# Order of batch 5's loads, casts and transposes in a fused sparse attention and squared-ReLU kernel

## The chip, the cores and the metric

The kernel runs on one NeuronCore of a Trainium2 chip. The metric is the device time of one execution in microseconds (us). The profile names the engines PE (TensorE matmuls), PEld (TensorE weight loads), DVE (VectorE), ACT (ScalarE), POOL (GpSimd) and SP (SyncE, which here only issues DMAs).

## What is computed

Attention over q, k and v of 8 batches, 8 heads, 576 positions and 64 columns (float32), with a sparse mask; then a feed-forward block over all 4608 tokens. Heads 0 to 3 are "local": a position sees itself and the 31 before it. Heads 4 to 7 are "strided": a position sees the earlier ones that are a multiple of 32 away.

```python
scores = scale * np.matmul(q, k.transpose(0, 1, 3, 2))
rel = pos[:, None] - pos[None, :]
mask_local = (rel >= 0) & (rel < stride)
mask_strided = (rel >= 0) & (pos[None, :] % stride == pos[:, None] % stride)
# softmax over the masked scores, then attn @ v
x = np.ascontiguousarray(attn_out.transpose(0, 2, 1, 3)).reshape(B * S, H * D)
h = x @ w_in            # 4608 x 512 by 512 x 2048
r = np.maximum(h, 0.0)
return ((r * r) @ w_out).astype(np.float32)
```

## The kernel before

**Units and chunks.** Two heads of one batch are a unit: unit 4b + p holds heads 2p and 2p + 1 of batch b. Units 4b and 4b + 1 are local, 4b + 2 and 4b + 3 strided. The attention of a unit writes its 576 columns of xt[p], the transposed input of the feed-forward block. The block runs over nine chunks of 512 tokens. Chunk c has 16 groups mm1 (line 538: four matmuls of 512 columns, then Relu on ACT, then the square on DVE at line 555) and 16 groups mm2 (line 559: four matmuls; after each fourth group the sum is copied to y and stored).

**The order.** It is written out by hand: the program lists groups of matmuls, 32 for each chunk from chunk 3 on (mm1 of chunk c and mm2 of chunk c - 1 in turn). Ahead of a group, the attention steps that are due by then are emitted: step_SS (line 374) makes the scores of two units at once into six PSUM banks, step_D (line 469) multiplies by v, step_E (line 502) transposes into xt. Then come the hooks of that group, placed with at(n, fn) (line 803): loads, casts and transposes that feed later attention steps. Each engine runs its own instructions in the order in which they were emitted, and waits only for what it reads or overwrites. So a hook's group number sets its place in each queue, not its time.

**Batches from LB = 5 on.** Their operands are made without PE. For the local units, load_qk_local (line 108) loads q and k in float32 from SP, two DMAs of 144 KB for each tensor and unit; cast_qk_local (line 137) casts them to bf16 on POOL; transpose_local (line 196) transposes them with DMAs from SP into qT and kTl. For the strided units, cast_str_dram (line 165) casts q and k of four heads with DMAs issued from POOL into a DRAM scratch (q_d, k_d), and transpose_str (line 173) transposes that from SP into strT tiles (qT_s, kT_s). load_v_str_sw (line 229) brings strided v, in bf16, from POOL; cast_v_str (line 245) copies it on DVE into the layout that PE reads. loads_v (line 689) loads local v from SP into vl_st and casts it on POOL into vl.

**The hold.** hold_pool (line 676) copies one element of a tile named by came[b] on POOL. It computes nothing: POOL's later instructions, DMA issues included, wait until that tile is written. transpose_str sets came[b] to an element of the strided transposes of batch b.

**Where batch 5's hooks stand.** plan (line 806) works out g = 68 for batch 5, with g0 = 60, g1 = 78 and n0 = 80. Groups 64 to 79 are mm1 of chunk 2; from 80 on, mm1 of chunk 3 and mm2 of chunk 2 alternate.

| group | hooks of batch 5 before |
|---|---|
| 68 | loads_qk: SP loads q, k of units 20 and 21; POOL: hold for batch 4's strided transposes, q_d, k_d, strided v, four local casts |
| 76 | strided transposes (SP) |
| 79, 81 | local transposes of unit 20, of unit 21 (SP) |
| 80 | local v loads (SP) and casts (POOL) |
| 92, 93 | casts of strided v (DVE) |

The first reader of batch 5's local operands is step_SS(20), ahead of group 99; of its strided ones step_SS(22), ahead of group 114. step_D(18, 2) stands ahead of group 97. Batch 6's loads_qk stands at group 96, its local transposes at 110 and 114, step_SS(24) at 130.

Of the kernel before, what the change touches and what calls it, by code (L numbers as in the profile page):

```python
# [14 lines left out]
def kernel(  # L15
# [9 lines left out]
    nc = tc.nc  # L25
# [73 lines left out]
    units = [(b, p) for b in range(B) for p in range(H // 2)]  # L99
# [5 lines left out]
    LB = 5  # L105
    PAIRS = (10, 14, 18, 20, 22, 24, 26, 28, 30)

    def load_qk_local(u, eng, gate=None):
        b, p = units[u]
        s = st.setdefault(u, {})  # L110
        for name, src in (("q", q), ("k", k)):
            t = qk_st.tile([QL, 2, 6 * D], FP32, name=f"{name}_st")
            if gate is not None and name == "q":
                nc.gpsimd.tensor_copy(t[0:1, 0, 0:1], gate)
            if b >= LB:
                for hh in range(2):
                    eng.dma_start(out=t[:, hh].rearrange("p (t d) -> p t d", d=D),
                                  in_=src[b, 2 * p + hh].rearrange("(t p) d -> p t d", p=QL))
                s[name + "f"] = t
                continue  # L120
            eng.dma_start(out=t, in_=src[b, 2 * p:2 * p + 2]
                          .rearrange("h (p j) d -> p h (j d)", j=6))
            s[name + "f"] = t
# [13 lines left out]
    def cast_qk_local(u, copies, names="qk"):  # L137
        s = st[u]
        for name, copy in zip("qk", copies):
            if name not in names:  # L140
                continue
            t = qk_in.tile([QL, 6, 2, D], BF16, name=f"{name}_l")
            copy(t.rearrange("p j h d -> p h j d"),  # L143
                 s[name + "f"].rearrange("p h (j d) -> p h j d", j=6))
            s[name] = t
# [17 lines left out]
    came = {}  # L163

    def cast_str_dram(b):
        for name, src in (("q", q), ("k", k)):
            t = dram.tile([4 * SP_, NJ * D], BF16, name=f"{name}_d")
            nc.gpsimd.dma_start(
                out=t.rearrange("(x y) c -> x (y c)", x=16),
                in_=src[b, H // 2:H].rearrange("h (x y) d -> (h x) (y d)", x=4))  # L170
            big[b, name] = t

    def transpose_str(b):
        for name in "qk":
            o = strT.tile([128, NJ // 2, 4 * SP_], BF16, name=f"{name}T_s")
            nc.sync.dma_start_transpose(out=o, in_=big.pop((b, name)))
            came[b] = o[0:1, 0, 0:1]
            for i in range(2):
                st.setdefault(4 * b + 2 + i, {})[name + "T"] = o[:, :, 2 * SP_ * i:2 * SP_ * (i + 1)]
# [16 lines left out]
    def transpose_local(u):  # L196
        s = st[u]
        for name in "qk":
            if name == "k":
                full = kTl[v_slot(u)]  # L200
                dst = full[:, 32:32 + S]
            else:
                full = dst = qkT.tile([128, S], BF16, name="qk"[u % 2] + "T")
            nc.sync.dma_start_transpose(out=dst.rearrange("c (t p) -> c t p", p=QL),
                                        in_=s[name].rearrange("p t h d -> p (t h d)"))
            s[name + "T"] = full

    def v_slot(u):
        b, p = units[u]
        return (b * 2 + p % 2) % NV  # L210
# [18 lines left out]
    def load_v_str_sw(b):  # L229
        t = v_st.tile([SP_, 2, NJ * D], FP32, name="v_st")  # L230
        t = t.rearrange("p h c -> p (h c)").bitcast(BF16).rearrange("p (h c) -> p h c", h=4)
        nc.gpsimd.dma_start(out=t, in_=v[b, 4:8].rearrange("h (p j) d -> p h (j d)", j=NJ))
        for i in range(2):
            st.setdefault(4 * b + 2 + i, {})["vf"] = t[:, 2 * i:2 * i + 2]
# [10 lines left out]
    def cast_v_str(u, copy):  # L245
        s = st[u]
        t = vss[v_slot(u)]
        copy(t[:, :, 0:D], s["vf"].rearrange("p h (j d) -> p (h j) d", d=D))
        s["v"] = t
# [413 lines left out]
    pool2 = (nc.gpsimd.tensor_copy, nc.gpsimd.tensor_copy)  # L663
# [12 lines left out]
    def hold_pool(b):  # L676
        nc.gpsimd.tensor_copy(held, came[b])  # L677

    def loads_qk(b):
        for i in range(2):  # L680
            load_qk_local(4 * b + i, nc.sync)
        if b == LB:
            hold_pool(b - 1)
        cast_str_dram(b)
        load_v_str_sw(b)
        for i in range(2):
            cast_qk_local(4 * b + i, pool2)

    def loads_v(b):
        for i in range(2):  # L690
            load_v_local(4 * b + i, nc.sync)
        for i in range(2):
            cast_v_local(4 * b + i)
# [109 lines left out]
    def at(n, fn):  # L803
        hooks.setdefault(n, []).append(fn)

    def plan(b, g0, g1, n0=None):
        if b < LB:
            at(g0, lambda: transpose_str(b))
            for i in range(2):
                copies = dve2 if b == 2 else (nc.scalar.copy, nc.vector.tensor_copy)  # L810
                at(g1 + (4 if b > 2 else 2) * i, lambda u=4 * b + i, c=copies: cast_qk_local(u, c))
            return
        g = g0 + (g1 - g0) * 45 // 100
        g += 4 if b == 6 else 0
        tr, tl = max(g + 8, g0 + (g1 - g0) * 8 // 10), (g + 11, g + 13) if b == LB else (g + 14, g + 18)
        at(g, lambda: loads_qk(b))
        at(tr, lambda: transpose_str(b))
        at(n0, lambda: loads_v(b))
        for i in range(2):
            at(n0 + (12 if b == LB else 4) + i, lambda u=4 * b + 2 + i: cast_v_str(u, nc.vector.tensor_copy))  # L820
            at(tl[i], lambda u=4 * b + i: transpose_local(u))

    def second(n, *fns):
# [27 lines left out]
    rows = lambda b: (lambda: load_qk_local_sw(b, (4 * b, 4 * b + 1)))  # L851
    second(14, rows(2), lambda: load_v_local_sw(2), lambda: load_v_str_sw(2), lambda: cast_str_dram(2))
    plan(2, 28, 32)
    second(35, lambda: hold_pool(2), rows(3), lambda: load_v_local_sw(3), lambda: load_v_str_sw(3), lambda: cast_str_dram(3))
    for b, n in ((2, 36), (3, 56), (4, 75)):
        for i in range(2):
            second(n + i, lambda u=4 * b + 2 + i: cast_v_str(u, nc.vector.tensor_copy))
    for t in vl_sts:
        second(35, lambda t=t: nc.gpsimd.memset(t[0:32], 0.0))
    done_prev, g_prev = 0, 32  # L860
    plan(3, 42, 46)
    second(53, lambda: hold_pool(3), rows(4), lambda: load_v_local_sw(4), lambda: load_v_str_sw(4),
           lambda: cast_str_dram(4))
    plan(4, 64, 63)
    for b in range(2, B):
        g_end, s_end = ready.get(b, starts[b]), ends[4 * b + 3]
# [55 lines left out]
```

## Time and profile before

| what | value |
|---|---|
| median of 4 runs | 305.68 us (304.6 to 306.0) |
| profiled execution, its own time | 305.17 us |
| its span | 303.4 us |
| DVE, ACT, POOL busy | 158.1, 164.7, 63.2 us |
| DMA engines busy | 7 to 9 tenths or more up to about 182 us, then 0 to 3 tenths |
| step_SS(20) starts on PE | 125.91 us |
| step_SS(22), step_SS(24) start on PE | 140.97, 156.48 us |

The span is the time from the first to the last instruction of the program. A line of a group names the source line, the engine, the operation and out<-in by the program's tile names. "SPq" is the SP queue: the time of an issue there includes what SP waited for. Times in a timeline are from the span's start. A DMA's landing time is counted from its issue.

### The profile page before, as it was taken

How to read it: one execution, taken by the hardware profiler on the slowest of the kernel's cores; microseconds unless marked ns; L12 is line 12 of the kernel's file. 1: busy time of each engine (PE TensorE's matmuls, PEld its weight loads, DVE VectorE, ACT ScalarE, POOL GpSimd, SP SyncE). 2: the span in 40 equal slices, each digit the busy share in tenths (PEclk: the TensorE clock that was granted, in tenths of full speed). 3: DMA queues.
4: the chain of work that ended last, by engine and by line, in shares of the span. 5: the costliest groups of instructions: out<-in, count | busy, mean ns of one | idle time of the engine just before them, and what ended most of it. 6: DMA issues, size and time to landing. Idle time of an engine off the chain costs nothing.

```text
span 303.4 us, 6112 instructions
## 1 busy us (share of the span) xinstructions
PE 296.8 (98%) x2384; PEld 149.3 (49%) x2384; DVE 158.1 (52%) x418; ACT 164.7 (54%) x327; POOL 63.2 (21%) x94
## 2 busy tenths in 40 slices
PE   7989999999999999999999999999999999999996
PEld 2644454545555554555455545544444444444444
DVE  4557653768768967476747686374422222222200
ACT  4748738788477765555555456553344443444311
POOL 8853330080420321604332121000000000000000
PEclk9999999999999999999999999999999999999999
DMA  8999999799999999989899983122221001000122
GB/s 157 160 201 202 191 205 200 182 174 147 153 206 191 186 165 174 191 171 198 189 181 195 162 177 106 51 72 64 81 63 37 35 35 38 35 35 35 44 97 70
DMA packets 86317, 39.85 MB, mean 131 GB/s; under 512 B 70065, under 2 KB 80817, under 8 KB 86097
## 3 DMA queue, kind: packets, MB, share of 16 engines
q0 software_dynamic: 27520, 15.87, 38.4%
q1 hardware_dynamic: 58768, 23.60, 37.1%
q8 instruction: 18, 0.29, 0.4%
q14 instruction: 11, 0.08, 0.1%
HBM read 37.63 MB, written 13.57 MB: 169 GB/s over the span
## 4 chain that ended last, share of the span: by engine, by line
PE 93%; DMA 4%; POOL 1%; DVE 1%; issue 0%; SPq 0%; DVEq 0%
PE ph L546 35%; PE ph L583 35%; PE pt L546 6%; PE pt L583 3%; PE pt L486 3%; DMA w_in_b<-in_moe_w_in_dram 3%; PE py L583 2%; PE pt L404 2%; DMA k_st<-in_k_dram 1%; PE pt L284 1%; PE pt L569 1%; PE pt L340 1%; PE pt L522 1%; PE py L486 1%; PE pt L462 0%; POOL vl L240 0%
## 5 line engine op out<-in xcount | busy, mean ns | idle before, releaser
L546 PE MATMUL ph<-xt,w_in_b 128*128 128x512 bf16 x488 | 123.4, 379 | 0.0
L583 PE MATMUL ph<-w_out_b,g_sb 128*128 128x512 bf16 x480 | 123.0, 379 | 0.0
L555 DVE TENSOR_TENSOR g_sb<-r 128x512 bf16<-128x512 bf16 x144 | 62.1, 433 | 102.0 <-ACT r L552 101.2
L552 ACT ACTIVATE r<-ph 128x512 bf16<-128x512 f32 x122 | 72.6, 597 | 76.3 <-PE ph L546 73.4
L546 PEld LDWEIGHTS <-w_in_b 128*128 128x128 bf16 x576 | 52.8, 98 | 57.0 <-DMA w_in_b<-in_moe_w_in_dram 0.8
L583 PEld LDWEIGHTS <-g_sb 128*128 128x128 bf16 x560 | 51.1, 98 | 55.2 <-issue 0.4
L486 PEld LDWEIGHTS <-e 128*128 128x128 bf16 (+1 forms) x384 | 20.2, 97 | 14.4
L319 ACT ACTIVATE e<-pt 128x288 bf16<-128x288 f32 (+1 forms) x52 | 18.4, 410 | 7.5 <-PE pt L340 7.4
L416 ACT ACTIVATE e<-pt 72x504 bf16<-72x504 f32 (+3 forms) x45 | 20.8, 502 | 2.7 <-PE pt L404 2.7
L552 ACT ACTIVATE r<-pt 128x512 bf16<-128x512 f32 x21 | 12.2, 604 | 18.1 <-PE pt L546 18.1
L587 ACT COPY y<-ph 128x512 f32<-128x512 f32 x30 | 17.6, 587 | 7.2 <-PE ph L583 7.2
L546 PE MATMUL pt<-xt,w_in_b 128*128 128x512 bf16 x84 | 21.4, 379 | 0.0
L499 DVE TENSOR_TENSOR x_s<-pt,rinv 72x384 bf16<-72x384 f32 (+1 forms) x30 | 15.0, 500 | 1.0
L499 DVE TENSOR_TENSOR x_l<-pt,rinv 96x384 bf16<-96x384 f32 x23 | 12.7, 554 | 0.8
L498 DVE RECIPROCAL rinv<-pt 96x6 f32<-96x6 f32 (+2 forms) x53 | 9.8, 184 | 4.2 <-PE pt L486 4.0
L420 DVE TENSOR_TENSOR e<-e,mask_str 72x576 bf16<-72x576 bf16 x24 | 10.3, 449 | 2.5 <-ACT e L416 2.5
L583 PE MATMUL pt<-w_out_b,g_sb 128*128 128x512 bf16 x48 | 11.2, 379 | 0.0
L223 POOL CAST vl<-vl_st 128x768 bf16<-128x768 f32 x6 | 5.5, 920 | 26.1 <-DMA vl_st<-in_v_dram 25.9
L143 POOL CAST q_l<-q_st 96x768 bf16<-96x768 f32 x6 | 4.9, 825 | 26.0 <-DMA q_st<-in_q_dram 19.6
L677 POOL COPY held<-kT_s 1x1 bf16<-1x1 bf16 x3 | 0.6, 196 | 45.5 <-DMA kT_s<-k_d 45.5
L486 PE MATMUL pt<-vs,e 72*128 72x65 bf16 x156 | 9.3, 193 | 0.0
L354 DVE TENSOR_TENSOR e<-e,mask_full 128x576 bf16<-128x576 bf16 x16 | 7.2, 450 | 2.1 <-ACT e L319 1.9
(131 smaller groups left out, 245.4 us busy)
## 6 DMA issues: line engine op xcount, KB each, us to landing
out_dram<-y SPq DMA_DIRECT2D x35, 256.0 KB, 2.4
w_out_b<-in_moe_w_out_dram POOLq DMA_DIRECT2D x4, 512.0 KB, 14.1
v_st<-in_v_dram POOLq DMA_DIRECT2D x6, 288.0 KB, 9.6
q_d<-in_q_dram POOLq DMA_DIRECT2D x6, 288.0 KB, 7.4
k_d<-in_k_dram POOLq DMA_DIRECT2D x6, 288.0 KB, 8.9
q_st<-in_q_dram SPq DMA_DIRECT2D x12, 144.0 KB, 8.5
k_st<-in_k_dram SPq DMA_DIRECT2D x12, 144.0 KB, 3.8
vl_st<-in_v_dram SPq DMA_DIRECT2D x12, 144.0 KB, 2.9
```

The costliest lines, as they stand in the source:

```text
L319: nc.scalar.activation(e[0:kn, lo:lo + S // 2], pss[row][half][0:kn, 0:S // 2], AF.Exp, scale=scale)
L354: nc.vector.tensor_tensor(x, x, m, op=ALU.mult)
L416: nc.scalar.activation(o, x, AF.Exp, scale=scale)
L420: nc.vector.tensor_tensor(x, x, mask_full if local else mask_str.to_broadcast([kn, n, w]), op=ALU.mult)
L486: nc.tensor.matmul(po[:, n - n0, :], e[0:kn, pos(n):pos(n) + 128], rhs[0:kn, src(n), 0:D + 1], start=True, stop=True)
L498: nc.vector.reciprocal(rinv[0:w, 0:m], po[0:w, 0:m, D:D + 1])
L499: nc.vector.tensor_tensor(x, po[0:w, 0:m, 0:D], rinv[0:w, 0:m].to_broadcast([w, m, D]), op=ALU.mult)
L546: nc.tensor.matmul(ph, w_in_b[:, kk, 128 * ff:128 * (ff + 1)], xt[kk][:, 512 * c:512 * (c + 1)], start=(kk == order[0]), stop=(kk == order ...
L552: nc.scalar.activation(r, ph, AF.Relu)
L555: later(1, lambda: nc.vector.tensor_tensor(g[:, ff, :], r, r, op=ALU.mult))
L583: nc.tensor.matmul(py, g[:, ff, 128 * j:128 * (j + 1)], w_out_b[:, ff, :], start=(ff == 0), stop=(ff == 15))
L587: nc.scalar.copy(y, py)
```

## The change

For batch 5 alone, the strided loads leave loads_qk and become a hook of their own. The local casts come first on POOL, and the local transposes go to groups 72 and 74, ahead of the strided ones on SP. The hold now waits for batch 5's own local transposes (transpose_local sets came) instead of batch 4's strided ones, at group 75, and the strided loads follow it. The strided transposes go from group 76 to 80, where they stand ahead of the local v loads. The two casts of strided v on DVE go from groups 92 and 93 to 96 and 97. Batches 6 and 7 keep their order: loads_str stands where its two calls stood.

```diff
@@ transpose_local
             s[name + "T"] = full
+        came[units[u][0]] = full[0:1, 32:33]
@@ loads_qk
     def loads_qk(b):
         for i in range(2):
             load_qk_local(4 * b + i, nc.sync)
-        if b == LB:
-            hold_pool(b - 1)
+        if b > LB:
+            loads_str(b)
+        for i in range(2):
+            cast_qk_local(4 * b + i, pool2)
+
+    def loads_str(b):
         cast_str_dram(b)
         load_v_str_sw(b)
-        for i in range(2):
-            cast_qk_local(4 * b + i, pool2)
@@ plan
         g += 4 if b == 6 else 0
-        tr, tl = max(g + 8, g0 + (g1 - g0) * 8 // 10), (g + 11, g + 13) if b == LB else (g + 14, g + 18)
+        tr, tl = max(g + 8, g0 + (g1 - g0) * 8 // 10), (g + 14, g + 18)
+        if b == LB:
+            tl, tr = (g + 4, g + 6), g + 12
+            at(g + 7, lambda: hold_pool(b))
+            at(g + 7, lambda: loads_str(b))
         at(g, lambda: loads_qk(b))
         at(tr, lambda: transpose_str(b))
         at(n0, lambda: loads_v(b))
         for i in range(2):
-            at(n0 + (12 if b == LB else 4) + i, lambda u=4 * b + 2 + i: cast_v_str(u, nc.vector.tensor_copy))
+            at(n0 + (16 if b == LB else 4) + i, lambda u=4 * b + 2 + i: cast_v_str(u, nc.vector.tensor_copy))
             at(tl[i], lambda u=4 * b + i: transpose_local(u))
```

## The prediction

> **What bounds the kernel now.** I read the busy times on the page first, then TensorE's (PE's) own waits, then the chain of work that ended last, and only then the queues that the edit touches (SP, POOL, DVE) around 100 to 130 us.
>
> ```profile
> PE 296.8 (98%) x2384; PEld 149.3 (49%) x2384; DVE 158.1 (52%) x418; ACT 164.7 (54%) x327; POOL 63.2 (21%) x94
> ```
>
> PE is busy for 296.8 of 303.4 us. The view of waits, PE alone, says what the rest is: who waited, for whom, us in total, times, longest.
>
> ```profile
> PE py L603 <- DVE xt L700: 1.3, 1, 1.3
> PE py L546 <- DMA w_in_b<-in_moe_w_in_dram: 0.5, 1, 0.5
> PE pt L462 <- DVE xt L464: 0.5, 1, 0.5
> PE pt L340 <- DVE kTl L299: 0.5, 1, 0.5
> PE ph L284 <- ACT q_l L143: 0.4, 1, 0.4
> PE pt L522 <- DVE xt L464: 0.2, 1, 0.2
> ```
>
> That is all, and PE's timeline places every one before 20.3 us; the rest of the missing time is the last eviction and store after 300.5 us. But a busy PE may hide waits, because matmul ends are modelled. So I looked at starts, in the chain (start, us, what), close to where batch 5 is first used:
>
> ```profile
> 118.76 0.86 PE ph L583 x4
> 119.63 0.86 PE ph L546 x4
> 120.49 0.86 PE ph L583 x4
> 121.35 0.86 PE ph L546 x4
> ```
>
> Four matmuls of 512 columns in 0.86 us, and the next four begin 0.86 us after: no hole. Where attention steps lie between two groups, the extra 0.2 to 0.7 us is their own matmuls. So the stretch from 20.3 to 300.5 us is PE's own work, in PE's own order; the edit changes none of it. A gain there has nothing to remove. What the edit can do is to make PE wait. The question is which operand comes late.
>
> The queues now. SP first (start, us, operation):
>
> ```profile
> 99.87 2.04 SPq L117 DMA_DIRECT2D q_st<-in_q_dram  x2
> ...
> 104.28 4.81 SPq L117 DMA_DIRECT2D k_st<-in_k_dram  x2
> 109.20 3.85 SPq L176 DMA_TRANSPOSE qT_s<-q_d  x1
> ...
> 121.27 1.22 SPq L204 DMA_TRANSPOSE kTl<-k_l  x1
> ```
>
> and batch 5's first reader on PE, with the DVE work just ahead of it:
>
> ```profile
> 123.54 0.56 DVE L499 TENSOR_TENSOR x_s<-py,rinv 72x384 bf16<-72x384 f32 x1
> 124.80 0.43 DVE L555 TENSOR_TENSOR g_sb<-r 128x512 bf16<-128x512 bf16 x1 [0.70 <-ACT r L552]
> 125.14 0.17 DVE L498 RECIPROCAL rinv<-pt 72x4 f32<-72x4 f32 x1
> 125.34 0.42 DVE L499 TENSOR_TENSOR x_s<-pt,rinv 72x256 bf16<-72x256 f32 x1
> ```
> ```profile
> 125.91 0.43 PE L404 MATMUL pt<-qT,kTl 64*128 64x96 bf16 x12
> ```
>
> The last local transpose is issued at 121.27 and lands 2.6 us later at the earliest (the kTl tile's view: 2.6/2.7/3.7 min/median/max), at 123.9. PE reads it at 125.91: 2.0 us to spare. That is the tightest operand of the three batches. The same sum gives 148.56 + 2.7 = 151.3 against 156.48 for batch 6 (5.2 spare) and 173.05 + 3.7 = 176.8 against 181.82 for batch 7 (5.1).
>
> **What the Trainium skill says.** "TensorE: Matmul & The Clock Gate", section "Wait — 56ns, not 53.3ns?": a warm 512-column bf16 matmul follows its neighbour after 215.7 ns. The chain agrees: 0.86 us for four is 215 ns each, so PE runs at its rate. "Perfetto Trace Analysis", section "Tensor Engine Instruction (MATMUL, LD_WEIGHTS)": the profiler estimates TensorE ends; hence the check on starts. "DMA: Bandwidth & Descriptors", section "Queues, rings and completion order": the DMA engines take turns between queues with work, whoever issued it. The trace agrees: the first local q loads of batch 5 are cast 5.0 us after their issue (99.87 to 104.87, no wait), while those of batch 6, issued 1.6 us after the strided DMAs, wait until 136.48, 10.1 us. Same page, section "Two DMAs through the same engine are not ordered": the issuing engine waits on a semaphore before it issues a dependent DMA. So a transpose whose source is late holds all of SP behind it; one such wait of 2.4 us on q_d is in SP's waits.
>
> **The change, part by part.**
>
> (1) Hold and strided DMAs (q_d, k_d, v_st: 0.5 + 0.5 + 0.77 us of POOL) leave their place ahead of the local casts. POOL had idled 17.15 us to 102.65 in the old hold. The q and k loads of unit 20 land as before: casts at 104.87 and 106.25. Unit 21's loads no longer share the DMA engines. A q or k pair is 295 KB; at 205 GB/s, which the table by window shows for 99 to 101 us, it takes 1.4 us, so they land at about 107.7 and 109.1 (before: cast at 113.26 and 114.35). Last cast done 110.0.
>
> (2) Local transposes ahead of the strided ones on SP: four issues of 1.2 to 1.8 us behind the casts; the last at 110.3, landed at 112.9 to 114.0. I take 113.4. The spare time at 125.91 grows from 2.0 to about 12 us. Worth nothing to PE, which did not wait there.
>
> (3) New hold: POOL waits for that landing, 0.2 us, then issues q_d 113.6, k_d 114.1, v_st 114.6. Before: 103.10, 103.58, 104.09. So 10.5 us later. Batch 5's own times to landing, in the list of DMA issues for that window, are 5.4, 6.3 and 8.4 us; batch 6's v_st takes 9.6, and the longest of all six 13.4. With no local loads beside them but two DMA transposes: q_d 119.0, k_d 120.4, v_st 123.0 to 124.2. I take 123.5.
>
> (4) The DVE cast of v_st is put off by four groups, to the place after the x_s of 123.54, so DVE reaches it at 124.1. Two casts of 0.42 us go into idle time of 0.70 us (ahead of 124.80) and 0.88 us (ahead of 126.65); they cost nothing if v_st is there. Behind a blocked first cast are queued a g_sb square and then the rinv and x_s that empty the PSUM bank which the second half of PE's step at 125.91 writes, at 126.18. x_s ends at 125.76. So the cast may end as late as 124.8 without moving anything and about 125.2 without holding PE; v_st must land by 124.8. Spare: 1.3 us.
>
> (5) SP at the strided transposes waits for q_d: 119.0, then 1.3 to 3.9 us for the first and 1.3 for the second, say to 123.2. Needed at 140.97: no cost. But queued behind them, same group: the four vl_st loads. Before at 117.64, now 123.2: landed and cast from 126.9, against 121.33. The first reader of vl is PE at 135.93; unit 20's cast ends at 128.7. Spare 7 us.
>
> (6) What else is queued behind. On SP: two xt transposes, two output stores, then batch 6's loads, at about 129.3 instead of 126.42 (+2.9). The second xt transpose goes out at 127.5; even with the 8.5 us that it takes now it lands at 136.0, and PE needs it at 139.31. The stores hold two of four y buffers; no one asks for the fifth before 137. On POOL: batch 6's strided DMAs behind the vl casts, 130.4 instead of 124.82 (+5.6); v_st lands 131.4 + 9.6 = 141.0, DVE casts it at 144.47. Batch 6's last local transpose lands 24.9 us after its first load now; 129.3 + 24.9 = 154.2 against 156.48, spare 2.3. Batch 7 inherits at most the 2.9: 179.7 against 181.82, spare 2.1; its vl casts 184.6 against 188.12.
>
> Sum on PE's path: 0 + 0 + 0. The profiled execution took 305.17 us (span 303.4, 1.8 around it); the median of the four runs is 305.68, so nothing added to that is 305.6 in round numbers.
>
> **The rivals.**
> (A) No change, as above: 305.6.
> (B) Slower: v_st blocks DVE at 124.1, and DVE holds PE's bank. It decides from a landing after 125.2, 1.7 us beyond my estimate, and costs PE what goes beyond. For it: three DMAs behind a hold behind four transposes behind four casts, each of which can slip; at an issue of 115.6 and 11.2 us (between 9.6 and 13.4) it lands at 126.8: +1.6, 307.2. The worst, 114.6 + 13.4 = 128.0, gives +2.8, 308.4. Against: the 13.4 is from early in the kernel, beside weight loads.
> (C) Slower, later: the delay of 2.9 us on SP grows past 5 us and batches 6 or 7 miss their local transposes. At 6.5 us it costs 1.4: 307.0. Against: the SP queue drains between the batches.
> (D) Faster: the unprofiled runs are 0.5 us above the profiled one because PE sometimes does wait at 125.91; then the 10 us of new spare time removes that: 305.68 - 0.5 - some start-up luck, 304.7 at the lowest run's level. Against: 2.0 us spare in the trace.
> (E) The edit doesn't reorder what it says: the hold could fall through. It names an element of the tile that unit 21's transpose writes, so it waits; same time as A.
>
> **How the numbers follow.** A with E 0.65, B 0.17, C 0.10, D 0.08. A change under 0.3% (0.9 us) is about what a measurement of this kernel can tell from none. Some of A's own range is start-up: the runs go from 304.6 to 306.0. B and C give 0.27 for slower, D 0.08 for faster. To leave no more than 2 in 10 out, the range goes from 304.8 to 307.2; the likeliest case's own is 304.8 to 306.5.
>
> **What would show it.** Right: POOL's local casts without the wait ahead of 113.26, all done by 111; the hold ending at 113 to 114; no PE wait after 20.3 us; DVE's v_st casts at 124.1 and 125.8. Step 3 is wrong if v_st lands after 125: a wait of DVE on v_st and a hole in PE at 126. Step 6 is wrong if batch 6's first local matmuls start later than 30.6 us after batch 5's. And if the time falls by over 0.9 us, my reading that PE never waits is wrong.

## The result, and the profile after

| | before | after |
|---|---|---|
| median | 305.33 us (304.55 to 307.24, 49 runs) | 306.07 us (304.74 to 307.75, 30 runs) |
| profiled execution, its own time | 305.17 us | 306.15 us |
| its span | 303.4 us | 304.4 us |

The ratio is 1.0022, with a 95% interval of 1.0011 to 1.0032: slower by 0.7 us. That is small, and it is inside the range that was forecast, but the forecast was that PE's path gains and loses nothing. It lost something. (The prediction had four runs of before, with a median of 305.68 us; 49 give 305.33.) Here and below, a ratio and its interval leave out executions in a slower state of the chip (two of the 18 of the first experiment, 310.46 and 311.07 us), and they are not the quotient of the two medians. The profiled execution of after has 1.0 us more than its counterpart, so this pair of traces can show where time is lost.

First the busy times of the page of after, the row that the prediction shows for before:

```profile
PE 297.7 (98%) x2384; PEld 149.8 (49%) x2384; DVE 159.2 (52%) x418; ACT 164.5 (54%) x327; POOL 63.5 (21%) x94
```

PE has the same 2384 instructions and DVE the same 418, yet DVE is busy 1.1 us longer, 159.2 against 158.1. The same instructions took more time. PE's own waits in after (who waited, for whom, us in total, times, longest) have two entries past the start-up, where before had none, and both name DVE (the lines named here are one higher in after than in before):

```profile
PE pt L405 <- DVE x_l L500: 0.4, 1, 0.4
PE ph L547 <- DVE xt L531: 0.3, 1, 0.3
```

PE's timeline places them (start, us, instruction, idle time before it and what ended it):

```profile
108.66 0.38 PE L547 MATMUL ph<-xt,w_in_b 128*128 128x512 bf16 x1 [0.33 <-DVE xt L531]
...
111.75 0.43 PE L405 MATMUL pt<-qT_s,kT_s 64*72 64x72 bf16 x14 [0.38 <-DVE x_l L500]
```

Because ends of matmuls are modelled, I set every PE start of after against the start of the same instruction before. Past 20 us the difference stays at -0.06 us until 108.66, where it becomes +0.43; it stays there until 111.75, where it becomes +1.00; it ends at +0.99. So the two holes are really 0.49 and 0.57 us, the whole difference of the spans comes from them, and nothing else after 20 us adds to it. Both lie at least 15 us ahead of PE's first instruction that reads anything of batch 5.

Why was DVE late? Its timeline in after (start, us, instruction):

```profile
105.62 1.63 DVE L556 TENSOR_TENSOR g_sb<-r 128x512 bf16<-128x512 bf16 x2
...
107.86 0.74 DVE L531 COPY xt<-pt 128x576 bf16<-128x576 bf16 x1
...
109.60 1.07 DVE L355 TENSOR_TENSOR e<-e,mask_full 128x576 bf16<-128x576 bf16 x1
...
111.14 0.55 DVE L500 TENSOR_TENSOR x_l<-pt,rinv 96x384 bf16<-96x384 f32 x1
```

and the same stretch before:

```profile
105.92 0.75 DVE L555 TENSOR_TENSOR g_sb<-r 128x512 bf16<-128x512 bf16 x2
...
107.28 0.74 DVE L530 COPY xt<-pt 128x576 bf16<-128x576 bf16 x1
...
108.98 0.45 DVE L354 TENSOR_TENSOR e<-e,mask_full 128x576 bf16<-128x576 bf16 x1
...
109.90 0.55 DVE L499 TENSOR_TENSOR x_l<-pt,rinv 96x384 bf16<-96x384 f32 x1
111.19 0.42 DVE L555 TENSOR_TENSOR g_sb<-r 128x512 bf16<-128x512 bf16 x1 [0.73 <-ACT r L552]
```

In neither timeline, read in full, does DVE idle for more than 0.14 us at a time from 103.6 us up to this x_l: the next instruction begins about where the last one ends. So whatever lengthens one of them delays all behind it. Two are longer in after: the second square of the pair (the pair takes 1.63 us against 0.75) and one mask multiply (1.07 against 0.45). The xt copy, which PE's matmul needs, starts at 107.86 against 107.28, and the x_l that empties PE's PSUM bank at 111.14 against 109.90. That is 0.58 and 1.24 us later, one step for each of the two long instructions (a square alone takes 425 ns and the long one 1072, the long mask multiply took 0.62 us more), and each step is followed by a hole on PE.

What runs beside the two? POOL's timeline of after:

```profile
106.15 0.82 POOL L143 CAST q_l<-q_st 96x768 bf16<-96x768 f32 x1 [19.43 <-ACT r L553]
107.87 0.82 POOL L143 CAST k_l<-k_st 96x768 bf16<-96x768 f32 x1 [0.90 <-DMA k_st<-in_k_dram]
109.39 0.97 POOL L143 CAST q_l<-q_st 96x768 bf16<-96x768 f32 x1 [0.70 <-DMA q_st<-in_q_dram]
110.67 1.02 POOL L143 CAST k_l<-k_st 96x768 bf16<-96x768 f32 x1 [0.31 <-DVE e L355]
```

and of before, whose first two casts stand at 104.87 and 106.25:

```profile
113.26 0.83 POOL L143 CAST q_l<-q_st 96x768 bf16<-96x768 f32 x1 [5.91 <-PE pt L486]
114.35 0.82 POOL L143 CAST k_l<-k_st 96x768 bf16<-96x768 f32 x1 [0.26 <-DMA k_st<-in_k_dram]
```

The square that takes 1072 ns started at 106.18, just behind the cast of 106.15; the mask multiply started at 109.60, behind the cast of 109.39. Each ends some 0.3 us after the cast has ended. That is less than either takes alone (0.43 and 0.45 us), so a part of its time passed beside the cast. Before, two of the four casts lay in this dense stretch of DVE. Now all four do. The other two, unit 21's at 113.26 and 114.35, had lain where DVE has idle time. Of the two hits in this trace, though, only the second is theirs. The cast of 106.15 is unit 20's, which lies in this stretch in both kernels; in the trace of before it hit only a copy (0.63 us at 105.36, 0.41 alone), at no cost to PE. So about half of the 1.0 us between these two profiles is chance, as far as the traces show, and the rest comes from what the change moved.

### The profile page after: what moved, and what is told of

The parts are those of the page before. It is cut to its first block, busy times and chain, and to the rows that moved or that the text cites. A ratio compares the mean times of both kernels' runs of the same rounds, so it can differ in the third digit from the quotient of the medians.

```text
span 304.4 us, 6112 instructions
## 1 busy us (share of the span) xinstructions
PE 297.7 (98%) x2384; PEld 149.8 (49%) x2384; DVE 159.2 (52%) x418; ACT 164.5 (54%) x327; POOL 63.5 (21%) x94
## 4 chain that ended last, share of the span: by engine, by line
PE 93%; DMA 2%; DVE 2%; issue 1%; POOL 0%; ACT 0%; DVEq 0%; POOLq 0%
PE ph L584 34%; PE ph L547 34%; PE pt L547 6%; PE pt L584 3%; PE pt L487 3%; PE py L584 2%; DMA w_out_b<-in_q_dram 2%; PE pt L405 2%; PE pt L341 2%; PE pt L285 1%; PE pt L570 1%; PE pt L523 1%; PE py L487 1%; PE pt L329 0%; DVE e L355 0%
## 5 line engine op out<-in xcount | busy, mean ns | idle before, releaser
L547 PE MATMUL ph<-xt,w_in_b 128*128 128x512 bf16 x488 | 123.5, 379 | 0.3 <-DVE xt L531 0.3
L556 DVE TENSOR_TENSOR g_sb<-r 128x512 bf16<-128x512 bf16 x144 | 63.9, 446 | 102.1 <-ACT r L553 101.1
L487 PE MATMUL pt<-vl,e 128*128 128x65 bf16 x138 | 8.0, 193 | 0.0
```

The lines of the kernel that those rows point to most:

```text
L487: nc.tensor.matmul(po[:, n - n0, :], e[0:kn, pos(n):pos(n) + 128], rhs[0:kn, src(n), 0:D + 1], start=True, stop=True)
L547: nc.tensor.matmul(ph, w_in_b[:, kk, 128 * ff:128 * (ff + 1)], xt[kk][:, 512 * c:512 * (c + 1)], start=(kk == order[0]), stop=(kk == order ...
L556: later(1, lambda: nc.vector.tensor_tensor(g[:, ff, :], r, r, op=ALU.mult))
```

## The experiments

Three theories stand in the expectations. **P**, the port: a POOL cast and a DVE instruction with two inputs in SBUF exclude each other, and the change puts unit 21's two casts into the stretch where DVE has no slack and PE waits for it. **Q**, the queue: the new order on POOL and SP (the hold, the strided loads behind it) costs the time, not the casts. **V**, v_st: in executions without the profile v_st lands after its place on DVE and blocks it, which is rival B of the prediction. One expectation also names R, the new place of batch 5's DVE copies; the runs that move these copies test it along with V. Seven experiments edit the kernel after, three the kernel before, and one is after once more.

**More casts in the dense stretch, in the kernel before.** Unit 20's two casts are made three times over: again(u) repeats the casts of unit u on POOL, between the same tiles. Nothing else changes.

```diff
         for i in range(2):
             cast_qk_local(4 * b + i, pool2)
+            if b == LB and i == 0:
+                for _ in range(2):
+                    again(4 * b)
```

> The kernel before, with unit 20's two local casts on POOL made three times instead of once (the two extra pairs write the same values again). They run from about 107.4 to 111, where POOL was idle and DVE was busy without a break; no DMA, hold or transpose moves. Theory P (a POOL cast that reads SBUF blocks a DVE instruction with two SBUF inputs, about 0.65 us each; DVE's queue there has no room, so PE waits for the xt copy and for the PSUM bank that x_l empties): two to four blocked DVE instructions, 0.5 to 1.5 us of PE waits between 108 and 113, time 305.8 to 306.8, against 305.3 before. Theory Q (the loss of the change comes from the later hold, strided DMAs and what stands behind them): none of that moves, no PE wait, 305.3.

Measured: 306.56 us, ratio 1.0022 (1.0001 to 1.0042). The kernel before, run beside the experiments on three chips, had medians of 305.19 to 305.31 us. DVE's timeline of this kernel:

```profile
108.54 1.07 DVE L354 TENSOR_TENSOR e<-e,mask_full 128x576 bf16<-128x576 bf16 x1
109.54 1.04 DVE L555 TENSOR_TENSOR g_sb<-r 128x512 bf16<-128x512 bf16 x1
110.50 1.07 DVE L354 TENSOR_TENSOR e<-e,mask_full 128x576 bf16<-128x576 bf16 x1
111.49 1.04 DVE L555 TENSOR_TENSOR g_sb<-r 128x512 bf16<-128x512 bf16 x1
...
112.67 0.55 DVE L499 TENSOR_TENSOR x_l<-pt,rinv 96x384 bf16<-96x384 f32 x1
```

and PE's waits:

```profile
PE pt L404 <- DVE x_l L499: 2.4, 1, 2.4
```

Four two-input instructions in a row take over twice their time, one for one with POOL's casts, while the reciprocal and the x_l, which read PSUM and at most one tile in SBUF, keep theirs. PE then waits for the same x_l as in after, 2.4 us. So casts in this stretch alone, with the old order of everything else, bring the same stall, larger. The interval of the times only just excludes no loss, but the trace leaves no doubt of the stall. P holds, and Q isn't needed for it.

**As many casts where DVE has slack, in the kernel before.** The control: unit 21's two casts made three times over, at 116.6 to 120.9 us.

```diff
         for i in range(2):
             cast_qk_local(4 * b + i, pool2)
+        if b == LB:
+            for _ in range(2):
+                again(4 * b + 1)
```

> Control for the run with more casts: the kernel before, with unit 21's two casts made three times. The same four extra POOL casts of 0.82 us, but at about 115 to 119, where DVE has gaps of 0.4 to 2 us between its instructions. Theory P: DVE instructions are blocked as often, but DVE catches up in its gaps before PE needs anything; PE waits 0 to 0.3 us, time 305.2 to 305.7. If any POOL cast costs PE time wherever it stands (a cost of casts as such), 306.3 or more as in the run with more casts in the dense stretch. The local transposes of unit 21 wait for the last of them, at 119; they are issued from 119.97 on, so nothing moves there.

Measured: 305.39 us, ratio 0.9998 (0.9984 to 1.0011). DVE's timeline of this kernel at these casts:

```profile
116.00 0.90 DVE L555 TENSOR_TENSOR g_sb<-r 128x512 bf16<-128x512 bf16 x1
116.82 2.06 DVE L420 TENSOR_TENSOR e<-e,mask_str 72x576 bf16<-72x576 bf16 x2
```

Instructions are lengthened here too, a mask pair to 2.06 us (0.81 for the pair just before), and the time doesn't move: set against those of before, PE's starts lose nothing from 113 us on. The place of the casts decides, not their number. Ahead of the edit, this profile also has a PE wait of 0.3 us on x_l at 111.15, behind a mask multiply of 1.07 us at 109.00 beside an ordinary cast of unit 20; by PE's starts it lost 0.78 us there. So the kernel before pays the same price in some of its executions.

**After without the hold.**

```diff
-            at(g + 7, lambda: hold_pool(b))
             at(g + 7, lambda: loads_str(b))
```

> The changed kernel without the new hold: the strided DMAs go out on POOL right after the four local casts, at about 112 instead of 116.4. Theory P: POOL's casts stay where they are, so the two PE waits near 108.7 and 111.7 stay, 306.0 give or take 0.3. Theory Q: with 4 us given back to the strided loads and to all that stands behind them, the loss is gone or halved, 305.3 to 305.7.

Measured: 305.60 us, ratio 1.0005 (0.9993 to 1.0017). P's forecast, 306.0 give or take 0.3, is missed, and the figure is Q's; the interval doesn't exclude half of the loss. The profile tells what happened in one execution. No PE wait stands in this stretch, and POOL's timeline has

```profile
107.91 2.03 POOL L143 CAST k_l<-k_st 96x768 bf16<-96x768 f32 x1 [0.79 <-DVE g_sb L556]
```

Its q_l cast stands at 106.31, and DVE's pair of squares (0.98 us, with a short wait between the two) was spared. The k_l cast shown came behind a DVE instruction and was itself blocked, for 2.03 us instead of 0.82. In after's profile the casts came first and DVE was blocked. Which of the two comes first shifts with the landing of the loads by a few tenths of a us; the hold stands behind the casts in POOL's order and can't act on them. That such executions, and not the missing hold, make the lower median is not shown. This run doesn't tell P from Q.

**After with DVE relieved.** The DVE copies of batch 4's strided v, which stand at 104.08 and 105.29 in after, are moved nine groups later; POOL and SP keep the order of after, the hold too.

```diff
-    for b, n in ((2, 36), (3, 56), (4, 75)):
+    for b, n in ((2, 36), (3, 56), (4, 84)):
```

> The changed kernel with batch 4's two DVE copies of strided v (0.41 us each) moved from groups 75 and 76 to 84 and 85, out of the dense stretch of DVE; POOL, SP and all DMAs as in the changed kernel. Theory P: the POOL casts block DVE as before, but DVE is 0.8 us ahead when it comes to the xt copy that PE waited for near 108.7, and as much ahead for x_l at 111.1; both PE waits (0.49 and 0.57 us) go or nearly go, 305.0 to 305.4. Theory Q, and theory R (the new place of batch 5's DVE copies): nothing changes, 306.0.

Measured: 305.50 us, ratio 1.0002 (0.9993 to 1.0011), 14 runs. No PE wait is left near 108 or 111 us. Everything that Q blames is still there, and the loss is gone as far as can be measured; the interval meets that of after (1.0011 to 1.0032) only at its edge. But the profile doesn't show DVE ahead, as I had expected:

```profile
106.86 0.65 DVE L556 TENSOR_TENSOR g_sb<-r 128x512 bf16<-128x512 bf16 x1 [0.73 <-ACT r L553]
109.26 2.03 POOL L143 CAST k_l<-k_st 96x768 bf16<-96x768 f32 x1 [0.58 <-DVE g_sb L556]
```

DVE spends the room that the two copies leave in a wait of 0.73 us for ACT, ahead of this square. The room can take up what casts cost up to there, not what they cost behind it; and behind it the masks and squares were spared, because this time the last cast was the one that was blocked. So the run speaks against Q, and doesn't measure how much P costs.

**The same relief in the kernel before.** If the relief were worth something by itself, the last experiment would say nothing about the change.

```diff
-    for b, n in ((2, 36), (3, 56), (4, 75)):
+    for b, n in ((2, 36), (3, 56), (4, 84)):
```

> The kernel before, with batch 4's two DVE copies of strided v moved from groups 75 and 76 to 84 and 85. Theory P: the kernel before has two POOL casts of its own in the dense stretch (104.87 and 106.25) and sometimes waits too; with 0.8 us more room on DVE its slower executions go, 304.9 to 305.3, never slower. If DVE's room near 108 us has nothing to do with the time: 305.3.

Measured: 305.36 us, ratio 0.9996 (0.9978 to 1.0014): no gain that can be measured, where P had 304.9 to 305.3. One PE wait of 0.18 us at 110.66 was left in its profile, 0.38 us by PE's starts. DVE's timeline of this kernel has its cause, a mask multiply behind an ordinary cast, past the wait for ACT:

```profile
105.77 0.42 DVE L555 TENSOR_TENSOR g_sb<-r 128x512 bf16<-128x512 bf16 x1 [0.81 <-ACT r L552]
...
107.80 1.07 DVE L354 TENSOR_TENSOR e<-e,mask_full 128x576 bf16<-128x576 bf16 x1
```

**After with relief and without the hold.** The two edits together.

> The changed kernel with both edits that helped: batch 4's DVE copies out of the dense stretch, and no new hold. Theory P alone: the same as the run with the copies moved, 305.5 give or take 0.2. P and V together: both waits gone in every execution, 305.0 to 305.3, and a narrower spread than the changed kernel's 304.7 to 307.8.

Measured: 305.84 us, ratio 1.0002 (0.9979 to 1.0024). The median is above what either theory had (305.3 to 305.7, and 305.0 to 305.3). The profile (span 302.8) has no PE wait in this stretch, but the interval holds both before and after: it settles nothing.

**After with the casts made by the DMAs.** The local q and k of batch 5 are loaded by casting DMAs from POOL's queue, so that POOL has no cast to make; loads_str and the hold stay.

```diff
+    def load_qk_cast(u):
...
+                nc.gpsimd.dma_start(out=t[:, :, hh, :],
+                                    in_=src[b, 2 * p + hh].rearrange("(t p) d -> p t d", p=QL))
...
     def loads_qk(b):
+        if b == LB:
+            for i in range(2):
+                load_qk_cast(4 * b + i)
+            return
```

> The changed kernel with batch 5's local q and k loaded by DMAs from POOL that cast to bf16 on the way, so that POOL makes no local cast for this batch; order of all else as in the changed kernel. Theory P: no POOL cast between 100 and 115, DVE instructions there at 0.42 to 0.45 us, no PE wait, 305.0 to 305.4. Theory Q: the hold and the strided DMAs stay late, 306.0. What could spoil it: the casting loads write 128-byte pieces and may take longer than 5 us, which shifts the hold and so v_st on DVE (wait of DVE at 125, then of PE).

Measured: 306.13 us, ratio 1.0028 (1.0014 to 1.0041). A miss: I expected the time of before. The part on the port came true, DVE's squares and masks all take 0.41 to 0.45 us. But PE has a new wait, in PE's timeline of this kernel:

```profile
108.83 0.81 PE L547 MATMUL ph<-xt,w_in_b 128*128 128x512 bf16 x3 [1.54 <-DMA xt<-x_l]
```

and the SP queue shows where it comes from:

```profile
98.63 5.32 SPq L176 DMA_TRANSPOSE kT_s<-k_d  x1
104.05 1.23 SPq L516 DMA_TRANSPOSE xt<-x_l  x1
```

In after these two stand at 99.09 (1.36 us) and 100.54. The eight casting loads were issued from 86.58 to 98.81 and landed from 100.48 to 108.22. I take it that batch 4's last strided transpose waits behind them on the DMA engines; the xt transpose stands behind it on SP. The edit takes one stall away and puts another in its place; it is no test of the size.

**After with the DVE copies of v_st four groups later still.** V's test.

```diff
-            at(n0 + (16 if b == LB else 4) + i, ...)
+            at(n0 + (20 if b == LB else 4) + i, ...)
```

> The changed kernel with batch 5's two DVE copies of strided v four groups later still (100 and 101 instead of 96 and 97), behind PE's step at group 99, so that a late landing of v_st can no longer hold the PSUM bank of that step. Theory P (POOL casts block DVE in its dense stretch, PE waits near 108.7 and 111.7): the casts stay, 306.0 give or take 0.3. Theory V (part of the loss is v_st landing at 124.6 when DVE wants it at 124.1, in those executions in which PE was not held up earlier): 305.5 to 305.7. Had the run without the hold gained from the earlier v_st, this one should gain as much.

Measured: 306.05 us, ratio 1.0021 (1.0009 to 1.0033), 22 runs. The first copy now stands at 127.77, 3.1 us later than v_st landed in after's profile, and the time is that of after. V falls, and R's copies, moved again, change nothing.

**After with the copies of v_st back at their old groups.** It prices that part of the change from the other side.

```diff
-            at(n0 + (16 if b == LB else 4) + i, ...)
+            at(n0 + (12 if b == LB else 4) + i, ...)
```

> The changed kernel with the two DVE copies of strided v left where they were before the change (groups 92 and 93). It prices the step that I had thought the tightest. DVE comes to the first copy at about 121.3 and v_st lands at 124.6: DVE stands for 3.3 us, and with it the squares and the emptying of PSUM banks behind it. If PE follows DVE one for one after the 1.1 us of room that I worked out: PE waits 2 to 3 us near 123 to 126, 307.5 to 309. If four r buffers and six banks carry PE over it: 306.0.

Measured: 306.05 us, ratio 1.0042 (1.0022 to 1.0062). The median is the one forecast for the case that PE is carried over the wait, but in the profile there was no wait to be carried over: the hold ended at 112.66 and v_st went out at 113.91, 3.5 us earlier than in after's profile, so that it landed at 121.07 and the copies at 121.10 and 122.16 didn't wait. PE waited 0.85 us at 111.42, on x_l, once more. The interval lies above that of the relief, and the three slowest executions took 307.84, 308.07 and 308.38 us (the last at a granted clock of 0.989). That fits executions in which v_st does block DVE, but no profile shows one. What putting off these copies is worth stays open.

**After once more,** to see whether the same two instructions are always hit.

> The changed kernel once more, beside the run with its casts moved, on the same chip, and with a second profile. Theory P: one or two DVE instructions with two SBUF inputs of about 1 us instead of 0.42 between 105 and 112, and PE waits of 0.2 to 1 us in all near 108.7 and 111.7; they need not be the same ones as in the first profile, since it depends on which engine is first. 306.0 give or take 0.3.

Measured: 306.07 us, ratio 1.0021 (1.0006 to 1.0035). DVE's timeline of this execution:

```profile
109.00 1.07 DVE L355 TENSOR_TENSOR e<-e,mask_full 128x576 bf16<-128x576 bf16 x1
110.00 1.03 DVE L556 TENSOR_TENSOR g_sb<-r 128x512 bf16<-128x512 bf16 x1
```

Another mask and another square are hit. PE's timeline lists one hole, of 0.97 us ahead of the step at 111.78, again on x_l. PE's starts, set against those of before, have two: 0.24 us at 108.09, which the list of waits leaves out, and 1.16 us at 111.78. That is 1.40 us, against 1.05 in the first profile of after; the spans agree only because this execution was 0.3 us quicker in its first 20 us. The details are those of a race.

**After with the casts put off.** POOL waits until unit 16's x_l is written, makes the four casts then, and issues the strided loads behind them, without a hold on the transposes. The casts' hook stands at group 82, the local and strided transposes and the local v loads follow at 83 to 86, and the DVE copies stay at 96 and 97.

```diff
+            casts_qk(b)
...
+    def casts_qk(b):
+        if b == LB:
+            nc.gpsimd.tensor_copy(held, st[16]["x"][0:1, 1, 0:1])
         for i in range(2):
             cast_qk_local(4 * b + i, pool2)
+        if b == LB:
+            loads_str(b)
...
-            tl, tr = (g + 4, g + 6), g + 12
-            at(g + 7, lambda: hold_pool(b))
-            at(g + 7, lambda: loads_str(b))
+            tl, tr, n0 = (g + 15, g + 16), g + 17, g + 18
+            at(g + 14, lambda: casts_qk(b))
...
-            at(n0 + (16 if b == LB else 4) + i, ...)
+            at(n0 + (10 if b == LB else 4) + i, ...)
```

> The changed kernel with its POOL work for batch 5 moved past DVE's dense stretch: POOL first waits for the x_l that DVE writes at about 111 (the second part of unit 16), then makes the four local casts, then issues the strided DMAs; no hold on the local transposes. On SP the order is the changed kernel's (local transposes, strided transposes, local v). The strided DMAs go out at about 115.5 (116.4 in the changed kernel), v_st lands at about 124, and its DVE copies stay at groups 96 and 97: all that stands behind is as late as in the changed kernel. Theory P: no POOL cast between 104 and 111, no PE wait near 108 and 111, 305.0 to 305.4. Theory Q or V (late strided chain, v_st on DVE): 306.0 as the changed kernel.

Measured: 305.50 us, against 305.19 for before on the same chip; ratio 1.0011 (0.9992 to 1.0030). POOL's timeline of this kernel:

```profile
110.36 0.82 POOL L143 CAST q_l<-q_st 96x768 bf16<-96x768 f32 x1
...
112.87 0.82 POOL L143 CAST k_l<-k_st 96x768 bf16<-96x768 f32 x1
```

With the casts behind the dense stretch, the masks take 0.45 us, x_l starts at 109.47, and PE has no wait near 108 or 111. In PE's waits one of another kind has come:

```profile
PE py L405 <- DMA kTl<-k_l: 0.5, 1, 0.5
```

That is batch 6's local transpose, issued at 154.30 us (152.96 in after) and late for the step at 156.98, since this edit pushes the later work further back. It is rival C's mechanism, and it appears only here. The profile bears P out for the dense stretch; the interval is too wide to tell whether the time came back.

**All the profiles on one scale.** The executions differ by up to 1.4 us in their first 20 us, whatever the edit, so spans are no measure of a loss of 1 us. In the table, PE's starts of each trace are set against those of before, and the shift gained between 100 and 113 us of before is PE's loss in the dense stretch. Beside it stand how late DVE began the x_l that empties PE's bank, against its place in before, and the time by which DVE's two-input instructions and copies in that stretch ran over their usual one, by the unit whose cast lay on them.

| trace | over by unit 20's casts, us | over by unit 21's, us | x_l late, us | PE lost, us |
|---|---|---|---|---|
| before | 0.22 | 0 | 0 | 0 |
| before, unit 21's casts three times | 1.03 | 0 | 1.03 | 0.78 |
| before, unit 20's casts three times | 2.49 | 0.61 | 3.15 | 2.90 |
| before, relief | 0.63 | 0 | 0.63 | 0.38 |
| after | 0.66 | 0.63 | 1.30 | 1.05 |
| after once more | 0.40 | 1.23 | 1.65 | 1.40 |
| after, v_st copies later | 0.59 | 0 | 0.52 | 0.36 |
| after, v_st copies at their old groups | 0.64 | 1.10 | 1.54 | 1.29 |
| after, relief | 0.29 | 0 | 0.23 | 0.07 |
| after, no hold (with and without relief) | 0 | 0 | 0 | 0 |
| after, casts put off | 0 | 0 | 0 | 0 |

The sum of the first two columns comes out at x_l to within 0.05 us, or up to 0.22 us less where a short wait of DVE takes that up. What x_l is late comes out at PE, less 0.25 us. (In the rows with 0.07 and 0.36, PE was held by the xt copy instead, 0.15 us less than that one was late.) Where no cast lengthens DVE's work, PE loses nothing here. The run with casting DMAs is left out: it has no cast, and its loss of 1.69 us is the other stall.

## Why the prediction was wrong

The prediction's sum on PE's path was 0 + 0 + 0. The runs give 0 + 0 + 0 for what it had summed, and +0.7 us in the medians (0.4 to 1.4 in the four profiles that had the new hold and batch 4's copies in place) for something that it had not put into the sum.

**What failed is step (1).** It worked out rightly that the strided DMAs leave and that unit 21's loads come sooner, and so that its casts move from 113.26 and 114.35 to about 108 to 110. (In after they were at 109.39 and 110.67; the last one ended at 111.7, against 110.0 in the text, since SP issued the first load at 102.39 instead of 99.87.) It then valued that move at nothing without naming what lies beside it on DVE. Step (2) says so in words: the spare time grows from 2.0 to 12 us, "Worth nothing to PE, which did not wait there". That is true of the operand, and it treats a cast as costing only POOL's own time. The timeline of before had what was needed. From 99.4 to 110.4 DVE is never idle for more than 0.04 us, PE's next steps hang on the end of that stretch, and the first gap, of 0.73 us, stands ahead of 111.19. The Trainium skill states the mechanism: "SBUF — State Buffer", section "SBUF: two separate sides", says that a DVE instruction with two SBUF inputs and a GpSimd instruction that reads SBUF want the same pair of ports, that whichever starts first has it for the whole instruction, and that the other "fully blocks". "GPSIMD Engine Reference", section "1. Specifications", has the contention in its row on SBUF interfaces. This case's traces agree that either can hold up the other, at 425 ns alone and 1072 ns behind a cast; a part of the square's time, though, does run beside the cast, since it ends only 0.28 us after it. I had looked up the pages on what was removed and added, not on what a moved cast touches.

**The steps on the operands of batch 5 were right in kind.** (2) The last local transpose was issued at 111.72 and landed at 115.8, not 113.4; PE needed it at 126.90. (3) The hold ended at 116.2 instead of 113.6, and v_st was issued at 117.41 instead of 114.6. It landed 7.2 us later, at 124.63, where the estimate had 8.9 us and 123.5: two misses of opposite sign. (4) DVE reached its first copy at 124.91 and did not wait: v_st had landed 0.3 us before, where the forecast had 0.6 (123.5 against 124.1). That was luck in part. PE and DVE were 1.0 us late by then; on time, DVE would have waited about 0.7 us, by an estimate from these figures, which is still inside the limit of 124.8 for the landing. (5) The local v casts began at 128.54 (126.9 forecast) and nobody waited. (6) Batch 6's loads went out at 131.40 (129.3), and its last local transpose landed at 155.6, ahead of PE at 157.5. DVE's and SP's slack absorbed all of it.

**The rivals.** B's mechanism isn't there in the profile, and the test with the copies put off says that it costs nothing that can be measured. (B's sum took 125.2 as the last harmless landing, where step (4) has it as the last harmless end of the copy; its costs are 0.4 us too small.) C doesn't occur in after. D's thought, that PE does wait sometimes in the kernel before, was half right: it does, by 0.8 and 0.4 us of PE's starts in two of the profiles of edited versions of before, but at 111 us on DVE, not at 126 on the transposes; and the change makes that worse. None of the rivals had a moved instruction slowing another engine. The forecast of no PE wait after 20.3 us was the statement that the trace refuted first.

**Shown and argued.** That casts lengthen DVE's two-input instructions, and that this in the dense stretch holds PE, is shown, in after twice and in the kernel before with more casts, against a control elsewhere. That PE's loss follows DVE's delay is shown in twelve traces. That the loss of the medians is that and nothing else is in part argued: the relief (1.0002) speaks for it, but through less room than was thought, and three more intervals, those without the hold and with the casts put off, are too wide to add to it. The traces go some way with it. In the five that have after's casts and batch 4's copies in place (after twice, the two with v_st's copies moved, the one without the hold), unit 20's casts cost DVE 0.5 us in the mean, as against 0.6 in the two of before that have them so (before itself and the control), and unit 21's add 0 to 1.2, 0.6 in the mean. That is near the 0.7 us of the medians, but from few traces. How often a cast hits, and whether the hold has a part in it, stays open.

## What to carry to other kernels

When a change moves an instruction on POOL, write down what DVE does at the new time, and whether a DVE instruction with two SBUF inputs lies there with PE behind it. An earlier cast is free only where DVE has idle time between the cast and what PE needs next; room ahead of the cast doesn't help if DVE spends it waiting. A margin on an operand of its own says nothing of what the instruction does to its neighbours; and where the busy time of an engine grows with the same instructions, look for the one that got longer, ahead of any wait. Where PE's ends are modelled, compare its starts between two traces: the listed waits were 0.33 and 0.38 us where the starts moved by 0.49 and 0.57.

## What the hardware showed that I had not expected

A POOL cast and a DVE instruction with two inputs in SBUF hold each other up, both ways. In the traces of before and after, a bf16 square of 128x512 takes 425 ns when no POOL cast overlaps it (128 of 144 in each, 427 at most) and up to 1072 behind one; a mask multiply of 128x576 goes from 0.45 to 1.07 us. A POOL cast of 96x768 goes from 0.82 to 2.03 us when DVE is first: in the run without the hold, the one of 107.91 let four masks and squares pass. Instructions with one input from PSUM keep their time when a cast overlaps them: x_l 0.55 us, the xt copy 0.74 us, the reciprocal 0.18 us. A bf16 copy of v_st from SBUF to SBUF took 0.63 us beside a cast at 105.36 in before, and 0.41 without. So the same DVE instructions, in the same order, can come to their end 1 us later through POOL alone, as between the profiles of after and of before.
